# The first eight pairs of tiles take the eight experts' weights where they were prepared in SBUF; the stores to DRAM stand behind

## Chip, cores and metric

One core of one Trainium2 chip. The metric is the device time of one execution in microseconds (us).

## What is computed

A convolution over 7 positions whose weights differ by token and head, and then, on its result, a layer of experts:

```python
w = softmax(weight_gen, axis=-1)                     # 8 x 3584 x 8 heads x 7
out[b, s, h] = sum_k w[b, s, h, k] * x_pad[b, s + k, h]
x = out.reshape(28672, 192)
active = x @ w_skip > 0
e = argmax(x[active] @ w_gate)                       # one of 8 experts
gate = softmax(x[active] @ w_gate)[e]
out[active] = x + gate * (relu(x @ w1[e]) @ w2[e])   # 192 -> 1024 -> 192
```

All is float32 at the kernel's borders. The experts' part runs in float16, each operand split into a high and a low half.

## The kernel before

The 28672 tokens are 16 chunks of 1792; a chunk is four steps. The main loop (`while n["V"] < NCHUNK ...`) takes some 70 steps, and in each it walks a string of tokens, `SEQ[k % 4]`, each of which issues a piece of work if its conditions hold. No scheduler reorders anything: each engine gets its instructions in the order in which the tokens issue them, and waits in that order.

- `a b` (`band`, L323, VectorE) build banded weights; `C G` (`conv`, L342, TensorE) convolve, in two halves; `c e` (`conv_out`, L349, ScalarE) copy the result from PSUM; `K` (`back`, L358, L361) transposes it and forms gate sums, in three PSUM tiles of a pool of three; `O` (`back_out`, L372, L374, ScalarE) copies these out. `O` stands first in a step and takes the `K` of the step before; between the two stands one `F`.
- `L l H R r W V` compute each token's expert and its place (`logits_out` is L389, `rank` L431) and `place` (to L470) writes the rows' addresses; `pop` in `F` then issues 16 scatters of the chunk to the experts' buckets in DRAM (`send`, L483, GpSimd). They wait for TensorE's progress (`scatter`).
- `P` (`prepare`) drives `prep_expert`: for each of 8 experts load two raw halves (L198), take the maximum on ScalarE (L207, whose throw-away output goes into the expert's own weight slot `wo`), reduce it across partitions on TensorE (L213, L219) and VectorE (L215 to L229), write float16 halves into `wo` (L235 to L243), and store them to `wsp` in DRAM by six transfers (L246 to L249). The third block of 1024 columns is moved between partitions by these stores.
- `M` (`assign_one`) picks for the next pair of tiles (256 rows) the prepared expert with most rows waiting; `PAIRS_AFTER` limits the pairs by the chunks that are scattered. `D` (`ahead`, `fetch`) reads the numbers back on SyncE, loads the rows (`xg`, L619) behind the chunk's scatters, and loads the expert's weights from `wsp` into a slot (`wst`, four of them, L631, three transfers).
- `F` (`advance`) runs the pair's layer in eight parts: `prep_rows` (L641 to L664) scales and transposes the rows, `up` (L676, four groups of ten matmuls) and `hh`, `hl` (L680, L686), `down` (L696, four groups of twelve), `finish` (L702) and scatters of the result (L707). A pair that is next starts LEAD = 5 ticks (one per `F`) after its fetch; an assignment is fetched BEHIND = 2 ticks after it was made. When none is ready the stream drains and starts again.

There are 57 pairs: 48 in the loop, 9 dealt at its end. Behind the loop a tail runs the pairs that are left. The slots, PSUM and DRAM tiles carry their dependencies automatically; a load from `wsp` at a register's address counts as touching all of it, so stores and loads of `wsp` wait for each other.

Of the kernel before, what the change touches and what calls it, by code (L numbers as in the profile page):

```python
# [20 lines left out]
P = 128  # L21
# [35 lines left out]
]  # L57
EARLY, EVERY = 5, 2
# [4 lines left out]
LEAD = 5  # L63
BEHIND = 2
# [11 lines left out]
def conv_moe_kernel(ctx, tc, x, wg, w_skip, w_gate, w, out):  # L76
# [34 lines left out]
    wsp = dram.tile([E, P, WC], F16, name="wsp")  # L111
# [30 lines left out]
    nc.vector.tensor_tensor(pick, pick, iof[:, 0:E].unsqueeze(1).to_broadcast([1, E, E]), op=ALU.add)  # L142
    ecap_i = cst.tile([P, E], I32, name="ecap_i")
# [31 lines left out]

    dummy = cst.tile([P, RW], F32, name="dummy")
# [11 lines left out]
    nc.vector.tensor_copy(heads[:, 0, :], iof[:, 0:E])  # L188
# [5 lines left out]
    nc.vector.memset(most[:, E:E + 1], E * TT * float(P) - 0.5)  # L194

# [5 lines left out]
    def prep_expert(e, raws):  # L201
# [18 lines left out]
        yield  # L220
        mv = st.tile([P, 2], F32, tag="wmv", name="wmv")
# [10 lines left out]
        bh, bl = wo[:, 2 * FF:5 * FF // 2], wo[:, 5 * FF // 2:3 * FF]  # L232
# [11 lines left out]
        yield  # L244
        for i in range(2):
            nc.sync.dma_start(wsp[e, 0:64, 2 * FF + i * FF // 2:2 * FF + (i + 1) * FF // 2], bh[64 * i:64 * (i + 1), :])  # L246
            nc.sync.dma_start(wsp[e, 64:P, 2 * FF + i * FF // 2:2 * FF + (i + 1) * FF // 2], bl[64 * i:64 * (i + 1), :])
        nc.sync.dma_start(wsp[e, :, 0:2 * FF], wo[:, 0:2 * FF])
        nc.sync.dma_start(wsp[e, :, 3 * FF:], wo[:, 3 * FF:])  # L249

    prepared, open_, prepares = [0], [0], [0]

    def prep_all():
        raws = [load_part(0, 0), load_part(0, 1)]
        yield
        for e in range(E):
            after = [load_part(e + 1, i) for i in range(2)] if e + 1 < E else []
            yield from prep_expert(e, raws)
            raws = after
            prepared[0] += 1  # L260
            yield
# [256 lines left out]
    def assign(T, F, final):  # L518
# [43 lines left out]
        nc.vector.tensor_scalar(so[:, :, 0], ef, float(E - 1), None, op0=ALU.min)  # L562
# [7 lines left out]
        todo.extend((so, i, T, None) for i in range(F))  # L570
        told.extend([tick[0] + BEHIND] * F)

    def assign_one(T):

        n = prepared[0]
# [4 lines left out]
        nc.vector.scalar_tensor_tensor(t[:, 0:E], t[:, 0:E], float(E), pick[:, n, :] if n < E else iof[:, 0:E],  # L580
# [19 lines left out]
        todo.append((so, 0, T, counted[0]))  # L600
        told.append(tick[0] + BEHIND)

# [8 lines left out]
    def fetch(so, i, T, upto):  # L611

        NT = P * T
        er = nc.values_load(so[0:1, i, 0:1], engines=[ET.SP], min_val=0, max_val=E - 1,
# [119 lines left out]
    def pairs():  # L734

        while True:
# [4 lines left out]
            if ready[0][3] + LEAD > tick[0] and not auto[0]:  # L741
                return
# [3 lines left out]
    def flow():  # L746
# [25 lines left out]
        while cur:  # L772
            py = ps_y.tile([P, 2, 256], F32, tag="py", name="py")
            new = None
            for f2 in range(NFB // 2):
# [16 lines left out]
                if new and f2 == 1:  # L792
                    next(new[1])
# [215 lines left out]
```

## Time and profile before

| | |
|---|---|
| three runs | 964.08, 965.21, 965.73 us; median 965.21 |
| profiled execution | 956.43 us, of which the span is 954.5 |
| mean granted clock of TensorE | 0.927 of 2.4 GHz |
| TensorE busy | 814.2 us (85%) |
| VectorE, ScalarE, GpSimd busy | 659.5 (69%), 474.3 (50%), 403.9 us (42%) |

The page and the timeline come from the profiled execution, which is 8.8 us shorter than the median of the runs. A busy share is a mean over stretches with different limits: TensorE is busy far less in the first third than after it.

### The profile page before, as it was taken

What the parts mean: (1) busy time and instruction counts of PE and PEld (TensorE: products, weight loads), DVE (VectorE), ACT (ScalarE), POOL (GpSimd) and SP (SyncE); (2) the same over time, 40 slices, a digit from 0 to 9 for tenths busy, and PEclk for the clock granted to TensorE, in tenths of its full rate; (3) what the DMA queues carried; (4) which work ended last, traced back from release to release, by engine and by line L of the source; (5) the groups of instructions that cost most, each with busy time, mean ns of one, the idle gap of its engine ahead of it and who ended that gap; (6) DMA issues with size and microseconds to landing.
All of it is one profiled execution on the core that took longest, in us unless ns stands there. A gap on an engine that the chain in (4) does not pass through costs nothing. (4 is left out here: it accounts for less than half of the span.)

```text
span 954.5 us, 36775 instructions
## 1 busy us (share of the span) xinstructions
PE 814.2 (85%) x15248; PEld 694.1 (73%) x15248; DVE 659.5 (69%) x1945; ACT 474.3 (50%) x1141; POOL 403.9 (42%) x415
## 2 busy tenths in 40 slices
PE   0567853778799997999899998999999899999997
PEld 0446633567587886888788786887888789899996
DVE  4888974746877785878686876687675566855553
ACT  0456655454555544555445463555555455455552
POOL 1008883243344536354626372545454353712122
PEclk9787775877799997999999999999999999999999
DMA  6588698897687569576868595768576559876540
GB/s 225 179 291 280 223 305 300 303 323 237 193 283 269 187 229 307 169 246 229 261 190 274 174 299 166 245 201 263 189 267 201 164 196 287 272 257 219 194 158 19
DMA packets 99176, 221.33 MB, mean 232 GB/s; under 512 B 16144, under 2 KB 54859, under 8 KB 97216
## 3 DMA queue, kind: packets, MB, share of 16 engines
q1 hardware_dynamic: 81248, 197.22, 62.2%
q0 software_dynamic: 17760, 21.75, 7.2%
q8 instruction: 120, 1.97, 0.8%
q14 instruction: 48, 0.39, 0.1%
HBM read 152.97 MB, written 77.80 MB: 242 GB/s over the span
## 5 line engine op out<-in xcount | busy, mean ns | idle before, releaser
L483 POOL DMA_INDIRECT bucket<-acc,ixi x256 | 279.2, 1091 | 320.9 <-DVE wst L229 68.0
L676 PE MATMUL ph<-xT,wst 128*128 128x256 f16 x2280 | 296.7, 279 | 20.2 <-DVE hl L686 12.8
L676 PEld LDWEIGHTS <-wst 128*128 128x128 f16 x2280 | 219.8, 100 | 59.5 <-issue 22.4
L680 ACT ACTIVATE hh<-ph 128x512 f16<-128x512 f32 x228 | 135.8, 595 | 243.3 <-PE ph L676 239.9
L686 DVE SCALAR_TENSOR_TENSOR hl<-ph,hh 128x512 f16<-128x512 f32 x228 | 155.8, 684 | 144.6 <-ACT hh L680 144.4
L696 PE MATMUL py<-wst,hh 128*128 128x192 f16 x1824 | 247.0, 248 | 0.0
L696 PE MATMUL py<-wst,hl 128*128 128x192 f16 x912 | 225.6, 247 | 2.8 <-issue 1.9
L707 POOL DMA_INDIRECT out_dram<-xg x114 | 117.1, 1027 | 225.5 <-DVE xg L702 171.7
L342 PE MATMUL bt<-bd,xt 64*32 64x56 f32 x8192 | 125.7, 232 | 59.3 <-DVE bd L323 27.9
L696 PEld LDWEIGHTS <-hh 128*128 128x128 f16 x1824 | 164.3, 99 | 15.8 <-issue 9.4
L342 PEld LDWEIGHTS bt<-bd,xt 64*32 64x32 f32 x8192 | 100.9, 113 | 92.2 <-issue 47.3
L323 DVE TENSOR_TENSOR bd<-rot,mask 128x896 f32<-128x896 f32 x128 | 137.0, 1080 | 8.8 <-DMA rot<-img 8.8
L696 PEld LDWEIGHTS <-hl 128*128 128x128 f16 x912 | 89.8, 98 | 3.4 <-issue 2.1
L664 ACT COPY xT<-pt 128x512 f16<-128x512 f16 x114 | 61.4, 590 | 57.2 <-PE pt L663 57.2
L702 DVE SCALAR_TENSOR_TENSOR xg<-py,fc,xg 128x192 f32<-128x192 f32 x114 | 42.2, 411 | 64.7 <-PE py L696 60.6
L349 ACT COPY xs<-bt 128x448 f32<-128x448 f32 x128 | 66.0, 539 | 37.0 <-PE bt L342 36.8
L358 PE MATMUL pa<-ident,xs 128*112 128x128 f32 x512 | 77.8, 298 | 1.6 <-ACT xT L664 1.1
L650 ACT ACTIVATE xs<-xg,rs 128x192 f16<-128x192 f32 x114 | 45.7, 449 | 44.1 <-DVE rs L647 31.0
L358 PEld LDWEIGHTS pa<-ident,xs 128*112 128x112 f32 x512 | 63.1, 147 | 5.1 <-ACT xT L664 2.8
L663 PE MATMUL pt<-ident,xs 128*128 128x128 f16 x456 | 41.7, 226 | 24.0 <-ACT acc L372 13.2
L372 ACT COPY acc<-pa 112x384 f32<-112x384 f32 x128 | 55.0, 481 | 1.6 <-PE pa L358 1.5
L663 PEld LDWEIGHTS <-xs 128*128 128x128 f16 x456 | 30.1, 100 | 31.1 <-DVE xs L656 19.7
(152 smaller groups left out, 734.3 us busy)
## 6 DMA issues: line engine op xcount, KB each, us to landing
wst<-wsp SPq DMA_DIRECT2D x114, 512.0 KB
wst<-wsp SPq DMA_DIRECT2D x57, 520.0 KB
xt<-in_x_dram SPq DMA_DIRECT2D x64, 384.0 KB
out_dram<-acc SPq DMA_DIRECT2D x16, 1358.0 KB
raw<-in_moe_w_dram SPq DMA_DIRECT2D x16, 768.0 KB
xg<-bucket SPq DMA_DIRECT2D x57, 194.0 KB
rot<-img SPq DMA_DIRECT2D x16, 448.0 KB
wt<-in_weight_gen_dram SPq DMA_DIRECT2D x16, 392.0 KB
```

The source lines that it names most:

```text
L323: nc.vector.tensor_tensor(bd.rearrange("p h (m u) -> p h m u", m=K), rot_[c][:, :, i0 * H:(i0 + 2) * H].rearrange("p m h -> p h m").unsque ...
L342: mm = nc.tensor.matmul(bt[a][GP * j:GP * (j + 1), c0:c0 + QH], xt[p0:p1, b0:b0 + GP], bd_[k, i // 2][p0:p1, i % 2 * H + h, :], start=True ...
L349: nc.scalar.copy(xs_[k][:, 2 * a:2 * a + 2, :], bt_[k][a][:, 0:2 * QB * QH].rearrange("p (x c) -> p x c", x=2))
L358: nc.tensor.transpose(pa[j][0:Q, x * P:(x + 1) * P], xs[:, x, j * Q:(j + 1) * Q], ident)
L483: i = nc.gpsimd.indirect_dma_start(out=bviews[t], out_offset=bass.IndirectOffsetOnAxis(ap=rt_[c][:, t:t + 1], axis=0), in_=acc_[c][:, t, : ...
L663: nc.tensor.transpose(pt[:, 2 * i2 + i, :], xs[:, t, i2, i * P:(i + 1) * P], ident16)
L664: nc.scalar.copy(xT[:, :, t * P:(t + 1) * P], pt)
L676: mm = nc.tensor.matmul(ph[:, fi * 2 * P:(fi + 1) * 2 * P], wt[:, a * FF + f0:a * FF + f0 + P], xT[:, cc, :], start=j == 0, stop=j == 4)
L680: nc.scalar.activation(hh, ph, AF.Relu)
L686: nc.vector.scalar_tensor_tensor(hl, ph, 0.0, hh, op0=ALU.max, op1=ALU.subtract)
L696: mm = nc.tensor.matmul(py[:, t, 0:D], l[:, a], w2v[:, f, r, :], start=f == 0 and t == 0 and j == 0, stop=f == NFB - 1 and j == 2, skip_gr ...
L707: i = nc.gpsimd.indirect_dma_start(out=oviews[nsc[0] % 8], out_offset=bass.IndirectOffsetOnAxis(ap=xg[:, t0 + t, D + 1:D + 2].bitcast(I32) ...
```

## The change

- The first eight assignments name experts 0 to 7 in order, whatever waits in the buckets (`only`), and their pairs use the slot in which that expert was prepared (`fresh`): no load. Experts 4 to 7 are prepared only when pair 0 to 3 is done with its slot (`spent`).
- A new token `s`, once a step from step 14 on, stores one prepared expert, by three transfers, to its own view of `wsp`. Later loads name the stores that they wait for. Four small transfers inside SBUF (from a scratch `low`) do the move between partitions.
- The maximum's throw-away output goes to a scratch `spare`; the slot is taken later.
- `O` stands right behind `K`.
- In a pair's second quarter the rows' low half (L653, L656) is issued before `hl` (L686), not behind it.
- The first pair waits longer: BEHIND 4 and LEAD 7 ticks. Preparation may run faster after step 14 (EVERY 3).

```diff
 SEQ = [
-    "O x F C a D F G w P L F l D c b T M P F e 2 P F H P F D P T M K F P",
+    "x F C a D F G w P L F l D c b T M P F e 2 P F H P F D P s T M K O F P",
...
-EARLY, EVERY = 5, 2
+EARLY, EVERY = 5, 3
+SLOTS = 4
+CUTS = ((0, 2 * FF), (2 * FF, 4 * FF), (4 * FF, WC))
-LEAD = 5
-BEHIND = 2
+LEAD, BEHIND = (5, 7), (2, 4)
...
-    wsp = dram.tile([E, P, WC], F16, name="wsp")
+    wsp = dram.tile([E * P, WC], F16, name="wsp")
+    wviews = dram_disjoint_views(wsp[:, :], E)
+    stored = []
...
+    nc.sync.dma_start(wsp[0:1, 6 * FF + 2:WC], zero[0:1, 0:15].bitcast(F16))
...
     def prep_expert(e, raws):
-        wo = sl.tile([P, WC], F16, tag="wst", name="wst", bufs=4)
         for i in range(2):
-            nc.scalar.activation(wo[:, 0:3 * FF // 2], raws[i], AF.Abs, accum_out=m[:, i:i + 1])
+            nc.scalar.activation(spare, raws[i], AF.Abs, accum_out=m[:, i:i + 1])
             yield
         yield
-        yield
+        if e < SLOTS - 1:
+            yield
...
         nc.tensor.matmul(pm[:, 2 * P:2 * P + 2], ones2, dg, start=True, stop=True)
         yield
+        wo = sl.tile([P, WC], F16, tag="wst", name="wst", bufs=SLOTS)
...
-        bh, bl = wo[:, 2 * FF:5 * FF // 2], wo[:, 5 * FF // 2:3 * FF]
+        low = sl.tile([P, FF], F16, tag="low", name="low", bufs=1)
+        bh, bl = low[:, 0:FF // 2], low[:, FF // 2:]
...
         for i in range(2):
-            nc.sync.dma_start(wsp[e, 0:64, ...], bh[64 * i:64 * (i + 1), :])
-            nc.sync.dma_start(wsp[e, 64:P, ...], bl[64 * i:64 * (i + 1), :])
-        nc.sync.dma_start(wsp[e, :, 0:2 * FF], wo[:, 0:2 * FF])
-        nc.sync.dma_start(wsp[e, :, 3 * FF:], wo[:, 3 * FF:])
+            half = slice(2 * FF + i * FF // 2, 2 * FF + (i + 1) * FF // 2)
+            nc.sync.dma_start(wo[0:64, half], bh[64 * i:64 * (i + 1), :])
+            nc.sync.dma_start(wo[64:P, half], bl[64 * i:64 * (i + 1), :])
+        fresh[e] = wo
+        unkept.append((e, wo))
+
+    def keep():
+        e, wo = unkept.pop(0)
+        to = wviews[e][e * P:(e + 1) * P, :]
+        stored.append([nc.sync.dma_start(to[:, c0:c1], wo[:, c0:c1]).ins for c0, c1 in CUTS])
...
         for e in range(E):
+            while e >= SLOTS and spent[0] <= e - SLOTS:
+                yield
...
-    def assign_one(T):
-        n = prepared[0]
+    def assign_one(T, own):
+        n = len(stored)
+        which = only[:, own, :] if own is not None else pick[:, n, :] if n < E else iof[:, 0:E]
...
-        told.append(tick[0] + BEHIND)
+        told.append(tick[0] + BEHIND[given[0] == 1])
...
+        if own is not None:
+            return T, fresh.pop(own), xg
-        wt = sl.tile([P, WC], F16, tag="wst", name="wst", bufs=4)
-        for c0, c1 in ((0, 2 * FF), (2 * FF, 4 * FF), (4 * FF, WC)):
-            nc.sync.dma_start(wt[:, c0:c1], wsp[ds(er, 1), :, c0:c1].rearrange("a p c -> p (a c)"))
+        wt = sl.tile([P, WC], F16, tag="wst", name="wst", bufs=SLOTS)
+        for c0, c1 in CUTS:
+            i = nc.sync.dma_start(wt[:, c0:c1], wsp[ds(er, P), c0:c1])
+            if paced[0]:
+                for j in chain(*stored[:most_e]):
+                    after(i, j, "the weights of an expert")
...
     def ahead(n):
-        while ... and fetched[0] - before[1] < 4 - (prepared[0] < E):
+        while ... and (todo[0][5] < prepared[0] if todo[0][5] is not None else prepared[0] == E and fetched[0] - before[1] < SLOTS):
...
+                if new and f2 == 1:
+                    next(new[1])
                 late.append((cur, py, f2, up_low(*h)))
...
-                if new and f2 == 1:
-                    next(new[1])
...
-        if ffn[0] is None and ready and ready[0][3] + LEAD <= tick[0] and START <= step[0]:
+        if ffn[0] is None and ready and ready[0][3] + LEAD[spent[0] == 0] <= tick[0] and START <= step[0]:
...
-                chores.append(assigned())
+                chores.append(assigned(given[0] - 1 if given[0] <= E else None))
+        elif t == "s":
+            if unkept and k >= FIRST:
+                keep()
```

How the order moves, in three places. First SyncE around the first pair's fetch (`xg<-bucket`); `wsp<-wst` is a store of weights, `wst<-wsp` a load, `xt` an input of the convolution, `rot` its weights. Before:

```order
L276 DMA xt_131<-in_x_dram 128x768
L316 DMA rot<-img_78 128x7x128
L614 TENSOR_LOAD bs
L616 TENSOR_LOAD bs
L619 ISA
L619 DMA xg<-bucket 128x2x194
L631 ISA
L631 DMA wst<-wsp 128x2048
L631 ISA
L631 DMA wst<-wsp 128x2048
L631 ISA
L631 DMA wst<-wsp 128x2080
```

Now:

```order
L267 DMA wsp<-wst 128x2048 x2
L267 DMA wsp<-wst 128x2080
L297 DMA xt_135<-in_x_dram 128x768
L337 DMA rot<-img_78 128x7x128
L639 TENSOR_LOAD bs
L642 ISA
L642 DMA xg<-bucket 128x2x194
L267 DMA wsp<-wst 128x2048 x2
L267 DMA wsp<-wst 128x2080
L297 DMA xt_136<-in_x_dram 128x768
```

The three loads behind the fetch are gone, and stores of experts 0 and 1 stand on its two sides. Further on the four transfers `wst<-low` of experts 4 to 7 each stand behind a pair's fetch.

ScalarE around the first pair, whose first instruction is the one that reads `xg`. Before:

```order
L372 COPY acc<-pa 112x2x192 x2
L374 COPY ls<-pl 128x224
L240 ACTIVATE wst<-raw,wsc 128x8x192
L641 ACTIVATE xs,S_2525<-xg 128x192 x2
L389 COPY L<-lt 112x4x2x9 x2
L349 COPY xs_2536<-bt 128x448
L650 ACTIVATE xs<-xg,rs 128x192 x2
L349 COPY xs_2536<-bt 128x448
L207 ACTIVATE wst,wm<-raw 128x1536 x2
L372 COPY acc<-pa 112x2x192 x2
```

Now:

```order
L410 COPY L<-lt 112x4x2x9 x2
L370 COPY xs_2494<-bt 128x448 x2
L393 COPY acc<-pa 112x2x192 x2
L395 COPY ls<-pl 128x224
L669 ACTIVATE xs,S_2559<-xg 128x192 x2
L448 ACTIVATE dl<-dl 112x128
L678 ACTIVATE xs<-xg,rs 128x192 x2
L463 COPY qf<-rk 128x136
L370 COPY xs_2668<-bt 128x448 x2
L692 COPY xT<-pt 128x4x128 x2
```

The copies of the logits, of the convolution and of the next `back` now stand ahead of the pair's first instruction, not behind it, and no preparation of an expert stands between.

VectorE in the second quarter of a pair (`xs<-xs` ends the rows' low half, `bd` is a band of the convolution). Before, and then now:

```order
L702 SCALAR_TENSOR_TENSOR xg<-py,fc,xg 128x192 x2
L686 SCALAR_TENSOR_TENSOR hl<-ph,hh 128x512
L653 SCALAR_TENSOR_TENSOR xs<-xg,rs,xs 128x192 x2
L656 COPY xs<-xs 128x2x64 x2
L323 TENSOR_TENSOR bd<-rot,mask 128x896
L686 SCALAR_TENSOR_TENSOR hl<-ph,hh 128x512
```

```order
L730 SCALAR_TENSOR_TENSOR xg<-py,fc,xg 128x192 x2
L681 SCALAR_TENSOR_TENSOR xs<-xg,rs,xs 128x192 x2
L684 COPY xs<-xs 128x2x64 x2
L714 SCALAR_TENSOR_TENSOR hl<-ph,hh 128x512
L344 TENSOR_TENSOR bd<-rot,mask 128x896
L714 SCALAR_TENSOR_TENSOR hl<-ph,hh 128x512
```

The first `hl` has moved behind the rows' low half.

On TensorE the groups of up and down matmuls stand in these steps (a step is counted from one `back` to the next); nine transposes of pairs and two groups of logits lie in steps 16 to 26 in both:

| step | 16 | 17 | 18 | 19 | 20 | 21 | 22 | 23 | 24 | 25 | 26 | sum | 30 | 31 |
|---|---|---|---|---|---|---|---|---|---|---|---|---|---|---|
| up, before | 3 | 3 | 3 | 3 | 0 | 4 | 3 | 4 | 3 | 3 | 4 | 33 | 1 | 2 |
| up, now | 1 | 3 | 4 | 3 | 4 | 1 | 2 | 3 | 4 | 3 | 4 | 32 | 2 | 1 |
| down, before | 0 | 3 | 4 | 5 | 0 | 1 | 4 | 3 | 3 | 4 | 3 | 30 | 3 | 0 |
| down, now | 0 | 2 | 3 | 4 | 3 | 4 | 0 | 3 | 3 | 4 | 3 | 29 | 4 | 0 |

From step 40 on the two orders are never more than a group or two apart.

## Rows read from the trace of the kernel before

**Rows 1.** The page: its first line.
```profile
span 954.5 us, 36775 instructions
```
**Rows 2.** Stretch, us, then busy PE, PEld, DVE, ACT, POOL (xcount); PEclk, DMA share, GB/s.
```profile
148.35:320.50 172.15, 132.69 (x2444) 108.53 (x2444) 116.90 (x336) 85.32 (x196) 61.68 (x67) 0.84 0.81 270
234.30:259.60 25.30, 17.87 (x379) 13.51 (x378) 21.66 (x71) 14.36 (x34) 9.76 (x11) 0.80 0.60 187
357.50:382.10 24.60, 19.15 (x381) 15.41 (x379) 12.77 (x38) 10.08 (x29) 14.51 (x14) 0.79 0.90 306
```
**Rows 3.** Timeline of TensorE, undisturbed work: start, us, line, [idle before <-releaser].
```profile
102.19 1.09 PE L358 MATMUL pa<-ident,xs 128*112 128x128 f32 x8
...
104.67 1.90 PE L342 MATMUL bt<-bd,xt 64*32 64x56 f32 x126 [0.66 <-ACT xs L349]
106.50 1.08 PE L358 MATMUL pa<-ident,xs 128*112 128x128 f32 x8
...
843.39 0.22 PE L663 MATMUL pt<-ident,xs 128*128 128x128 f16 x1
...
844.19 1.25 PE L676 MATMUL ph<-xT,wst 128*128 128x256 f16 x10
845.29 0.33 PE L696 MATMUL py<-wst,hh 128*128 128x192 f16 x2
...
846.28 1.25 PE L676 MATMUL ph<-xT,wst 128*128 128x256 f16 x10
```
**Rows 4.** Timeline of TensorE around the first pairs and after the dry spell.
```profile
129.39 2.10 PE L342 MATMUL bt<-bd,xt 64*32 64x56 f32 x128 [4.54 <-DMA xt<-in_x_dram]
...
145.35 3.19 PE L381 MATMUL lt<-four,ls 128*112 128x32 f32 x16 [0.48 <-ACT acc L372]
...
158.13 0.97 PE L361 MATMUL pl<-xs,gt 128*32 128x224 f32 x8 [7.84 <-ACT L L389]
163.27 0.27 PE L663 MATMUL pt<-ident,xs 128*128 128x128 f16 x1 [4.17 <-ACT acc L372]
...
198.22 2.29 PE L676 MATMUL ph<-xT,wst 128*128 128x256 f16 x10 [2.57 <-ACT xs L349]
...
371.45 0.97 PE L663 MATMUL pt<-ident,xs 128*128 128x128 f16 x8 [3.59 <-ACT acc L372]
```
**Rows 5.** Timeline of SyncE around the first fetch.
```profile
144.32 0.63 SPq L316 DMA_DIRECT2D rot<-img  x1
154.45 0.41 SPq L619 DMA_DIRECT2D xg<-bucket  x1
```
**Rows 6.** Timeline of GpSimd: chunk 2's last scatter.
```profile
151.30 0.94 POOL L483 DMA_INDIRECT bucket<-acc,ixi  x1 [0.30 <-issue]
```
**Rows 7.** Timeline of ScalarE around the first pairs.
```profile
157.05 0.36 ACT L641 ACTIVATE xs<-xg 128x192 f16<-128x192 f32 x1 [9.65 <-DMA xg<-bucket]
...
195.69 1.48 ACT L207 ACTIVATE wst<-raw 128x1536 f16<-128x1536 f32 x1 [6.26 <-PE py L696]
```
**Rows 8.** Waits of TensorE, 120 to 270 us: total us, times, longest.
```profile
PE ph L676 <- DVE hl L686: 4.6, 3, 2.7
...
PE pl L361 <- DVE wmv L222: 4.2, 3, 2.1
...
PE pm L219 <- DVE wd L217: 2.2, 3, 0.9
```
**Rows 9.** Sum of the five stretches of 139.6 to 252.2 at 1.2 GHz.
```profile
sum 64.90, PE 43.59 PEld 32.80 DVE 40.80 ACT 29.81 POOL 17.30; mean PE 8.72 PEld 6.56 DVE 8.16 ACT 5.96 POOL 3.46
```
**Rows 10.** Waits of TensorE in the tail, 775 to 950 us.
```profile
PE pt L663 <- DVE xs L656: 3.3, 17, 0.3
```
**Rows 11.** Timeline of VectorE in a step of the steady loop.
```profile
501.39 0.74 DVE L653 SCALAR_TENSOR_TENSOR xs<-xg,rs,xs 128x192 f16<-128x192 f32 x2
502.16 0.29 DVE L656 COPY xs<-xs 128x128 f16<-128x128 f16 x2
```
**Rows 12.** Timeline of TensorE in the same step.
```profile
501.53 1.26 PE L676 MATMUL ph<-xT,wst 128*128 128x256 f16 x10 [0.62 <-DVE hl L686]
```

More of the change, by code (lines that the diff above doesn't have):

```diff
@@ L142, in conv_moe_kernel @@
     nc.vector.tensor_tensor(pick, pick, iof[:, 0:E].unsqueeze(1).to_broadcast([1, E, E]), op=ALU.add)
+    only = cst.tile([1, E, E], F32, name="only")
+    nc.gpsimd.memset(only, -BIG)
+    nc.gpsimd.affine_select(out=only, in_=only, compare_op=ALU.not_equal, fill=0.0, base=0,
+                            pattern=[[1, E], [-1, E]], channel_multiplier=0)
+    nc.vector.tensor_tensor(only, only, iof[:, 0:E].unsqueeze(1).to_broadcast([1, E, E]), op=ALU.add)
     ecap_i = cst.tile([P, E], I32, name="ecap_i")
@@ L194, in conv_moe_kernel @@
     nc.vector.memset(most[:, E:E + 1], E * TT * float(P) - 0.5)
+    spare = cst.tile([P, 3 * FF // 2], F16, name="spare")
     def load_part(e, i):
@@ L561, in assign @@
         yield
-        nc.vector.tensor_scalar(so[:, :, 0], ef, float(E - 1), None, op0=ALU.min)
+        nc.vector.tensor_scalar(so[:, :, 0], ef, float(E - 1), float(P), op0=ALU.min, op1=ALU.mult)
         yield
@@ L569, in assign @@
         yield
-        todo.extend((so, i, T, None) for i in range(F))
-        told.extend([tick[0] + BEHIND] * F)
-    def assign_one(T):
-        n = prepared[0]
+        todo.extend((so, i, T, None, E, None) for i in range(F))
+        told.extend([tick[0] + BEHIND[0]] * F)
+    def assign_one(T, own):
+        n = len(stored)
+        which = only[:, own, :] if own is not None else pick[:, n, :] if n < E else iof[:, 0:E]
         w = float(P * T)
@@ L579, in assign_one @@
         yield
-        nc.vector.scalar_tensor_tensor(t[:, 0:E], t[:, 0:E], float(E), pick[:, n, :] if n < E else iof[:, 0:E],
+        nc.vector.scalar_tensor_tensor(t[:, 0:E], t[:, 0:E], float(E), which,
                                        op0=ALU.mult, op1=ALU.add)
@@ L599, in assign_one @@
         yield
-        todo.append((so, 0, T, counted[0]))
-        told.append(tick[0] + BEHIND)
+        todo.append((so, 0, T, counted[0], n, own))
+        told.append(tick[0] + BEHIND[given[0] == 1])
     def together(*gs):
@@ L609, in together, with fetch @@
                     gs.remove(g)
-    def fetch(so, i, T, upto):
+    def fetch(so, i, T, upto, most_e, own):
         NT = P * T
-        er = nc.values_load(so[0:1, i, 0:1], engines=[ET.SP], min_val=0, max_val=E - 1,
+        if own is None:
+            er = nc.values_load(so[0:1, i, 0:1], engines=[ET.SP], min_val=0, max_val=(E - 1) * P,
                             skip_runtime_bounds_check_because="clamped to the experts on the chip")
@@ L725, in ahead @@
     def ahead(n):
-        while len(ready) < n and todo and (told[0] <= tick[0] or auto[0]) and (todo[0][3] is not None or not unsent) and fetched[0] - before[0] < XG and fetched[0] - before[1] < 4 - (prepared[0] < E):
+        while len(ready) < n and todo and (told[0] <= tick[0] or auto[0]) and (todo[0][3] is not None or not unsent) and fetched[0] - before[0] < XG and (todo[0][5] < prepared[0] if todo[0][5] is not None else prepared[0] == E and fetched[0] - before[1] < SLOTS):
             fetched[0] += 1
@@ L740, in pairs @@
                 return
-            if ready[0][3] + LEAD > tick[0] and not auto[0]:
+            if ready[0][3] + LEAD[0] > tick[0] and not auto[0]:
                 return
@@ L837, in chosen, with assigned @@
         n["h"] += 1
-    def assigned():
-        yield from assign_one(TT)
+    def assigned(own):
+        yield from assign_one(TT, own)
         asked[0] -= 1
```

6 lines of the change are left out of this document (2 added, 4 removed), and 6 rows, old and new, of the table SEQ.

## The prediction, made before the changed kernel ran

> **What bounds the kernel now.** I read the page first, then TensorE's busy time by stretches, then its timeline where stretches are thin, then the rows of whoever it waited for. All sums are against the profiled execution: 956.4 us, of which the span is 954.5 [rows 1]; the median of the runs shown is 965.2, 8.8 above it, and I add 8.8 at the end.
>
> A step of the main loop is, on TensorE, the stretch from one `back` (L358) to the next. Undisturbed work has fixed prices [rows 3]: a step with no pair in it takes 106.50 − 102.19, less 0.66 idle, 3.65 us; one group of ten up matmuls 845.29 − 844.19 = 1.10; one group of twelve down matmuls 846.28 − 845.29 = 0.99; a pair's transposes 844.19 − 843.39 = 0.80; the logits 3.19 at 1.2 GHz [rows 4], so 1.6 at 2.4.
>
> The stretch 148.35 to 320.50 (steps 16 to 26) is where the pairs begin and the experts 4 to 7 are prepared between them. It lasts 172.15 us at a granted clock of 0.84 [rows 2]. By the table of groups its work is 11 × 3.65 + 33 × 1.10 + 30 × 0.99 + 9 × 0.80 + 2 × 1.6 = 40.2 + 36.3 + 29.7 + 7.2 + 3.2 = 116.6 us. So **55.5 us are lost there**. The reader is to see four kinds of loss in the rows:
> - The entrance. SyncE issued its last transfer at 144.32 and stood until 154.45 before the first pair's rows [rows 5], because that fetch waits for the scatters of chunk 2, and GpSimd's last one began at 151.30 [rows 6]. ScalarE stood 9.65 us at L641 for those rows [rows 7], and behind it stood the copies that TensorE needed: 7.84 us idle before L361, then 4.17 before the pair's transposes for a copy of L372 [rows 4].
> - ScalarE stood 6.26 us at L207 for a pair's down matmuls [rows 7]: the throw-away output of the maximum goes into a weight slot, which that pair still held. TensorE then lost 2.57 to L349, queued behind it [rows 4].
> - A drain between pairs: 25.30 us in steps 20 and 21 [rows 2].
> - The clock: 64.9 us of 139.6 to 252.2 went at 1.2 GHz, with TensorE busy for 43.59 of them [rows 9].
>
> **The change, part by part.** *Loads and stores.* Eight fetches of weights (3 transfers each) go; the eight stores become 3 transfers instead of 6, behind the pairs, and four small copies inside SBUF take the place of those of the third block. I cost the traffic itself at nothing on the path, because no row of TensorE names a weight load; the work that hides it is the stream of up and down matmuls. What it can free is the one wait of a convolution for `xt`, 4.54 us [rows 4], when loads, stores and scatters overlapped. Bounds 0 and 4.5; I take **3**, nearer to the row, since three experts' stores now stay away until step 14.
>
> *Steps 16 to 26.* By the table the change issues 32 up and 29 down groups here, 114.5 us of work by the same prices; the 2.1 us less come later and cancel. What stays lost:
> - Entrance: the scatters are neither moved nor fewer, so the rows cannot be there before about 157 [rows 5, 6, 7]. Behind them stand a few small steps, between 2 us and the 6.2 from 157.05 to 163.27 [rows 4, 7]; I take 3, since the order now puts the copies of L389 and L349 ahead of the wait. From 148.35 to 160.2 is 11.9, with 3.65 of work: 8 lost, and 6 more for the half clock that follows. **14.**
> - The drain, now between pairs 3 and 4 (steps 21 and 22, while expert 4 is prepared in the slot that pair 0 leaves). I price it by the one before: 25.3 less its work, 2 × 3.65 + 4 × 1.10 + 0.99 + 2 × 0.80 = 14.3. **11.**
> - The preparation on TensorE's path: 4.2 and 2.2 us for three experts [rows 8], 2.1 each, four experts. **8.5.**
> - Waits for `hl`: 4.6 [rows 8], as they are. **4.6.**
>
> Together 38 of 55.5, so the gain is **17**. From below it is 0 (each wait finds a successor); from above 38 (all but the drain and a bare entrance of 6 go).
>
> A rule to weigh here: in the rows, 43.59 us of busy time at 1.2 GHz would be 21.8 at 2.4, so the clock alone can give back at most 21.8 [rows 9], part of which is in my 17. The Trainium skill's "TensorE: Matmul & The Clock Gate" (HAM oscillation — how this bites in real kernels) counts the penalty as the whole throttled time × (1 − 1.2/2.4). By it an estimate for the 64.9 us is 32.5, and with that in place of the 17 the sum would end 15 us lower; the trace speaks against the full figure, since TensorE was idle for a third of that time.
>
> *Copies right behind transposes.* `back_out` follows `back` at once. Beside the 4.17 above, the transposes after the dry spell at 357.5 waited 3.59 for such a copy [rows 4]. Those two steps took 24.60 [rows 2] for 2 × 3.65 + 3 × 1.10 + 3 × 0.99 + 0.80 + 1.6 = 16.0 of work. The order keeps the dry spell (3 up and 4 down groups), so I take **4**, the wait and little of the clock; bounds 0 and 8.6.
>
> *The low half ahead of `hl`.* In the second quarter of a pair VectorE now runs L653 and L656 before L686. In the tail this ends the wait of the transposes for `xs`: 3.3 us in 17 waits [rows 10]; **3**, bounds 0 and 3.3. In the main loop it is a cost. Where the third up group stands between the halves of a convolution it waits for that very `hl` (0.62 at 501.53 [rows 12]), which now ends 502.16 + 0.29 − 501.39 = 1.06 later [rows 11]. In the order of the change five such groups follow after step 23: **−5**; bounds 0 and −9, if other pairs join.
>
> *The rest.* One more constant, a few set-up instructions and one tiny store at the start: **−0.5**, bounds 0 and −1. Views, scratch and the address in rows instead of experts are free; pairs 0 to 7 even save one register load each.
>
> Sum: 3 + 17 + 4 + 3 − 5 − 0.5 = 21.5. 956.4 − 21.5 = 934.9; with 8.8, **944**.
>
> **The rivals.**
> - *Only the named waits go* (the scratch's 2.57, part of 4.17; 5 of my 17, and nothing at the dry spell). VectorE, busy 116.90 of 172.15 us [rows 2], carries the same preparation later and takes over. Sum 3 + 5 + 3 − 5 − 0.5 = 5.5: **960**. For it: the entrance is set by scatters. Against it: ScalarE's two stalls, 9.65 and 6.26, leave work queued that nothing else held. Chance 0.18.
> - *The clock stays up* from the first pair on: with 38 in the stretch and 8.6 at the dry spell the sum is 47, so **918**. For it: the clock was 1.2 GHz just where the waits stood. Against it: the drain and the entrance remain. Chance 0.06. It is the case nearest to what that rule of the Trainium skill (same page and section) would give.
> - *Slower: SyncE holds back the copies of the third block.* In the order, each expert's four copies stand behind a pair's fetch. If a fetch waits for scatters as the first one did (144.95 to 154.45, 9.5 us [rows 5]), expert and pair are late by that, for four experts 38 us: 21.5 − 38 = −16.5, so **982**. It decides once more than two of the four fetches stand that long, 2.3 × 9.5 being the gain. Against it: later pairs are told only after the chunk's last scatter was issued. Chance 0.10.
> - *No effect* (the loss stays 55 us, the steps merely change places): 965. Chance 0.04.
>
> **How the numbers follow.** The forecast has 0.62. The range of 924 to 963 takes in its own bounds where most of them lie (20 us to either side) and the first rival; it leaves out the clock's rival, the slower one and no effect, 0.20. Two parts in a thousand, about 2 us, are what a measurement can tell from no change. Faster: 0.62 × 0.97 + 0.18 × 0.9 + 0.06 = 0.82. Slower: 0.10 and a little of the forecast's worst end, 0.12. Within: 0.06.
>
> **What would show it.** In the changed profile: ScalarE's maximum (before L207) waits for no down matmul; no wait of transposes for L372's copies; steps 16 to 26 take about 155 us; one drain between pairs 3 and 4, with 1.2 GHz; in the tail no wait of the transposes for `xs`. I am wrong if the first pair's rows arrive well before 155 us, if the clock stays at 2.4 GHz from the first pair on, or if SyncE's copies of the third block stand behind a fetch.

## The result, and the profile after

The changed kernel took **948.73 us** (median of six runs, 946.41 to 960.81), beside 960.88 for the kernel before: a ratio of 0.988 [0.984, 0.992]. Ratios compare fast runs alone, and the run of 960.81 was a slow one. Measured again, with the profile that is read below, it was 953.75 beside 962.93: 0.990 [0.986, 0.993]. So it is faster, by 9 to 12 us where the sum had 21. The experiments ran on three chips. On that of the first four (this second measurement among them) the kernel before took 962.93 us, on that of the next four 962.16, so times of these eight are set side by side. On the third chip, where the last four ran, it took 1120.23 us, some 16% more; times of that chip are compared among themselves only, and with the others by their ratios to before.

The profiled execution of the change took 955.03 us, 1.3 above its median. That of before (956.43) lay 6.5 *below* the 962.93 of its runs beside the second measurement, so the two traces differ by less than the kernels do. I therefore read them by stretches. "Step k" is the stretch from one `back` on TensorE (now L379) to the next, counted from 0. The version "without own slots" is an experiment below; its profiled execution (966.08) is near its own median, and so is that of the best version (942.54), which is an experiment too.

| TensorE, us | before | change | change without own slots | best version |
|---|---|---|---|---|
| to step 16 | 148.4 | 144.5 | 153.9 | 146.9 |
| steps 16 to 26 | 172.1 | 164.7 | 166.3 | 158.6 |
| steps 27 to 47 | 266.0 | 272.5 | 272.0 | 262.0 |
| steps 48 to 62 | 182.6 | 193.3 | 193.8 | 192.6 |
| from step 63 to the span's end | 185.4 | 178.1 | 178.4 | 180.5 |
| span | 954.5 | 953.1 | 964.4 | 940.6 |

The change is 11.3 us ahead at the end of step 26 (309.2 against 320.5), loses that and more from there to step 62, and wins 7.3 in the tail. Of the 11.3, 2.1 is work that comes later (32 up and 29 down groups are issued by then, 33 and 30 in before; 30 and 27 in the best version, whose 158.6 is to be read so). First the page of the change, then its stretches, with the same columns as [rows 2], which the first and the last of them answer:

```profile
span 953.1 us, 36734 instructions
```
```profile
144.50:309.20 164.70, 128.51 (x2426) 105.18 (x2426) 114.36 (x329) 91.62 (x202) 69.51 (x73) 0.85 0.73 242
213.40:247.90 34.50, 26.33 (x602) 21.35 (x600) 26.48 (x78) 19.78 (x40) 7.39 (x8) 0.95 0.70 245
309.20:581.70 272.50, 249.76 (x4874) 212.96 (x4873) 198.09 (x596) 135.05 (x341) 129.55 (x126) 0.96 0.70 226
337.60:367.60 30.00, 25.17 (x576) 21.45 (x574) 18.35 (x54) 10.59 (x24) 19.05 (x18) 0.93 1.00 343
581.70:775.00 193.30, 176.96 (x3408) 151.72 (x3407) 129.21 (x409) 96.17 (x248) 87.65 (x89) 0.98 0.64 209
```

The stretches of before that are not in [rows 2]:

```profile
320.50:586.50 266.00, 247.72 (x4852) 210.43 (x4851) 194.97 (x589) 131.66 (x340) 128.60 (x126) 0.96 0.70 229
586.50:769.10 182.60, 172.31 (x3387) 147.97 (x3386) 127.42 (x407) 93.01 (x243) 85.81 (x87) 1.00 0.66 219
```

In steps 16 to 26 TensorE's idle time (stretch less busy) went from 39.5 to 36.2 us, and the granted clock from 0.84 to 0.85: nearly nothing of either. In 48 to 62 the change has 6.0 us more idle time and a clock of 0.98 where before had 1.00.

Now the entrance of the change, on GpSimd, SyncE, ScalarE and TensorE, which answers [rows 4 to 7]:

```profile
154.79 0.94 POOL L504 DMA_INDIRECT bucket<-acc,ixi  x1 [0.30 <-issue]
```
```profile
141.08 0.92 SPq L337 DMA_DIRECT2D rot<-img  x1
157.16 0.42 SPq L642 DMA_DIRECT2D xg<-bucket  x1
```
```profile
159.88 0.36 ACT L669 ACTIVATE xs<-xg 128x192 f16<-128x192 f32 x1 [12.05 <-DMA xg<-bucket]
```
```profile
141.62 3.09 PE L402 MATMUL lt<-four,ls 128*112 128x32 f32 x16 [1.49 <-ACT acc L393]
...
149.32 1.02 PE L363 MATMUL bt<-bd,xt 64*32 64x56 f32 x64
161.88 0.29 PE L691 MATMUL pt<-ident,xs 128*128 128x128 f16 x1 [11.54 <-ACT xs L678]
```

The form of the wait is new, its length is not: where before stood 7.84 and 4.17 us for copies that were queued behind the rows, the transposes now stand 11.54 us for the rows themselves. The fetch (157.16) still follows the last scatter (154.79) at once, and that scatter begins 3.5 us later than in before, though step 16 begins 3.9 earlier. So the first transposes come at 161.88 where they came at 163.27. Then the waits of TensorE from 120 to 270 us [rows 8], and in the tail [rows 10]:

```profile
PE pt L691 <- ACT xs L678: 14.0, 2, 11.5
PE pm L230 <- DVE wd L228: 6.9, 3, 4.3
...
PE bt L363 <- DVE hl L714: 2.5, 1, 2.5
...
PE ph L704 <- DVE hl L714: 1.8, 1, 1.8
...
PE pl L382 <- DVE wmv L234: 1.2, 1, 1.2
```
```profile
PE pt L691 <- DVE xs L684: 0.7, 1, 0.7
```

### The profile page after: what moved, and what is told of

Its sections match the earlier page's. It is cut to its first block, busy times and chain, and to the rows that moved or that the text cites. A ratio compares the mean times of both kernels' runs of the same rounds, so it can differ in the third digit from the quotient of the medians.

```text
span 958.9 us, 36734 instructions
## 1 busy us (share of the span) xinstructions
PE 819.6 (85%) x15248; PEld 701.5 (73%) x15248; DVE 660.9 (69%) x1946; ACT 479.5 (50%) x1141; POOL 409.6 (43%) x417
## 5 line engine op out<-in xcount | busy, mean ns | idle before, releaser
L504 POOL DMA_INDIRECT bucket<-acc,ixi x256 | 283.7, 1108 | 283.6 <-PE bt L363 71.6
L704 PE MATMUL ph<-xT,wst 128*128 128x256 f16 x2280 | 297.6, 279 | 23.5 <-DVE hl L714 13.6
L704 PEld LDWEIGHTS <-wst 128*128 128x128 f16 x2280 | 220.1, 100 | 63.6 <-issue 23.8
L724 PE MATMUL py<-wst,hh 128*128 128x192 f16 x1824 | 251.5, 251 | 0.0
L724 PE MATMUL py<-wst,hl 128*128 128x192 f16 x912 | 227.9, 250 | 0.2 <-DVE hl L714 0.2
L363 PE MATMUL bt<-bd,xt 64*32 64x56 f32 x8192 | 128.6, 234 | 67.8 <-DVE bd L344 28.0
L724 PEld LDWEIGHTS <-hh 128*128 128x128 f16 x1824 | 166.3, 100 | 16.1 <-issue 7.7
L379 PE MATMUL pa<-ident,xs 128*112 128x128 f32 x512 | 79.1, 302 | 6.4 <-issue 5.1
L379 PEld LDWEIGHTS pa<-ident,xs 128*112 128x112 f32 x512 | 64.3, 149 | 10.0 <-issue 5.6
L691 PE MATMUL pt<-ident,xs 128*128 128x128 f16 x456 | 37.1, 225 | 14.8 <-ACT xs L678 11.5
L669 ACT ACTIVATE xs<-xg 128x192 f16<-128x192 f32 x114 | 40.2, 360 | 11.4 <-DMA xg<-bucket 11.3
```

The source lines that it names most:

```text
L363: mm = nc.tensor.matmul(bt[a][GP * j:GP * (j + 1), c0:c0 + QH], xt[p0:p1, b0:b0 + GP], bd_[k, i // 2][p0:p1, i % 2 * H + h, :], start=True ...
L379: nc.tensor.transpose(pa[j][0:Q, x * P:(x + 1) * P], xs[:, x, j * Q:(j + 1) * Q], ident)
L504: i = nc.gpsimd.indirect_dma_start(out=bviews[t], out_offset=bass.IndirectOffsetOnAxis(ap=rt_[c][:, t:t + 1], axis=0), in_=acc_[c][:, t, : ...
L704: mm = nc.tensor.matmul(ph[:, fi * 2 * P:(fi + 1) * 2 * P], wt[:, a * FF + f0:a * FF + f0 + P], xT[:, cc, :], start=j == 0, stop=j == 4)
L724: mm = nc.tensor.matmul(py[:, t, 0:D], l[:, a], w2v[:, f, r, :], start=f == 0 and t == 0 and j == 0, stop=f == NFB - 1 and j == 2, skip_gr ...
```

## Experiments

My theory after the first reading: own slots bring the gain at the first pairs, and the other edits move the places where the order leaves TensorE without a pair. The rival: each edit acts by the waits that it removes. What the order gives can be counted before any run. Groups of ten up matmuls in each of steps 16 to 37:

```
before             3 3 3 3 0 4 3 4 3 3 4 3 4 3 1 2 4 3 4 3 4 3
change             1 3 4 3 4 1 2 3 4 3 4 3 4 3 2 1 4 3 4 3 4 3
without own slots  1 3 4 3 1 2 4 3 4 3 4 3 4 3 2 1 4 3 4 3 4 3
before, O moved    3 4 3 2 1 4 3 4 3 4 3 4 3 3 0 4 3 4 3 4 3 4
change, O back     0 4 3 4 3 2 0 4 3 4 3 3 4 3 4 3 4 3 3 4 3 4
O back, prep early 0 4 3 4 3 3 3 0 4 3 4 3 3 4 3 4 3 4 3 3 4 3
O back, LEAD 5     3 3 3 4 3 0 3 3 3 4 3 4 3 4 1 2 3 4 3 4 3 4
```

A dry spell is a step or two in which the order has few groups or none. Each row has one in steps 19 to 23. All but two rows have a second one in steps 30 and 31. The best version below has the row of `O` back.

**The change again** (no edit).

> The changed kernel once more, beside the others, for a second profile. Theory (the gain arises in steps 16 to 26, is given back in part in the main loop by waits for hl, and comes again in the tail): ratio to before about 0.988, steps 16 to 26 some 8 us shorter than before, a pair of the tail 8.77 us instead of 9.13, and in 385 to 775 us some 16 us of TensorE's waits for hl where before had 9. Rival (what was lost after step 24 in the first profile was chance stalls with no releaser, the issue waits): the waits for hl fall back to 9 us and the main loop takes no longer than before.

Measured: 953.75 (ten runs), 0.990 [0.986, 0.993]. The theory held: steps 16 to 26 are 7.4 us shorter than before, a pair of the tail takes 8.77 us instead of 9.13, and TensorE's waits for `hl` between 385 and 770 us are 16.5 us where before had 9.0.

**`hl` first everywhere.** The low half of the rows goes back behind `hl`, in the loop and in the tail:

```diff
-                if new and f2 == 1:
-                    next(new[1])
...
+                if new and f2 == 1:
+                    next(new[1])
```

> The change without its low half ahead of hl: hl first again, in the loop and in the tail. Theory: the order costs about 10 us in the main loop (waits for hl 16.5 against 9.0 us) and gives 0.36 us for each of 17 pairs of the tail, 6 us; without it the time is about 4 us below the change, 944 to 946 where the change has 948.7. Rival (the order costs nothing in the loop): 6 us above the change.

Measured: 953.13, 0.992 [0.987, 0.996]: neither 4 us below the change nor 6 above it, but the same. The trace shows both effects, and they cancel. Its steps 48 to 62 and its tail, where the change has 193.3 and 178.1 us:

```profile
578.40:766.60 188.20, 177.74 (x3410) 152.09 (x3408) 128.28 (x408) 96.36 (x248) 86.60 (x89) 0.98 0.65 214
766.60:951.20 184.60, 172.29 (x1859) 159.16 (x1856) 105.39 (x350) 89.49 (x222) 60.20 (x64) 0.99 0.59 196
```

**Low half first in the tail alone:**

```diff
-                if new and f2 == 1:
+                if new and f2 == 1 and auto[0]:
...
+                if new and f2 == 1 and not auto[0]:
+                    next(new[1])
```

> The low half ahead of hl in the tail alone, hl first in the main loop. Theory: both gains, some 10 us below the change, 938 to 941. Rival (no cost in the loop): the same time as the change within 2 us.

Measured: 952.53, 0.988 [0.984, 0.992]. The change's waits of TensorE between 385 and 770 us, then this version's:

```profile
PE ph L704 <- DVE hl L714: 10.5, 9, 1.9
PE bt L363 <- issue: 8.9, 4, 3.1
PE bt L363 <- DVE hl L714: 6.0, 6, 1.2
```
```profile
PE bt L363 <- issue: 11.5, 4, 3.8
PE ph L704 <- DVE hl L714: 4.2, 8, 0.9
PE bt L363 <- DVE hl L714: 2.9, 6, 0.8
```

The waits for `hl` fall from 16.5 to 7.1 us, as the order says, and of the 10 us that I expected nothing is seen beyond the interval; 2.6 us come back as waits without a releaser. In steps 48 to 62 this version is 3.2 us shorter than the change (190.1), in steps 27 to 47 it is 2.1 longer (274.6). Neither of the two versions differs from the change beyond its interval.

**`O` back.** The copies stand at the start of the next step again, in all four rows of `SEQ`; all else as changed:

```diff
-    "x F C a D F G w P L F l D c b T M P F e 2 P F H P F D P s T M K O F P",
+    "O x F C a D F G w P L F l D c b T M P F e 2 P F H P F D P s T M K F P",
```

> The change with the copies of back_out at the start of the next step again, as before. Theory (they removed 4.2 + 3.6 us of waits of transposes and free PSUM earlier): 4 to 8 us above the change. Rival (right behind the transposes ScalarE itself stands for TensorE, 10.4 us of idle time before L393 in the first profile against 1.5 before, and holds back what is behind): the same as the change or up to 5 us below it.

Measured: **945.98**, 0.984 [0.981, 0.988]; 7.8 us below the change on the same chip, where even the rival had at most 5. Between the transposes of pairs 10 and 11 now lie 13.0 us, where the change has 30.0. Steps 27 to 47, in which that spell lay, took 266.3 us instead of 272.5, with three more up groups in them.

**`O` moved, alone.** The kernel before, with `O` behind `K`; the diff is the one above read backwards.

> The kernel before with one edit: the copies of the convolution's transposed rows (O) stand right behind the transposes (K), where the change puts them, and not at the start of the next step. Taken back in the changed kernel, this edit gained 7 us (946 against 953). Theory: it is a loss wherever it stands, since it moves the point in the step at which the order opens the next pair by a third of a step, so that the spell without a pair at steps 31 and 32 becomes a whole step; the time is 2 to 8 us above before's, ratio 1.002 to 1.008. Rival: alone it frees the transposes of their wait for the accumulator copies (3.6 us at 371 and 4.2 us at 163) and costs nothing else: ratio 0.995 to 0.998; the loss in the changed kernel was then the meeting with the own slots.

Measured: 973.57, **1.011 [1.007, 1.015]**: slower than before by 10 to 11 us, more than the theory had. So this edit is a loss on either kernel. The reason that the theory gives is not borne out. In the order the edit does empty a whole step (step 30: no group) where before had two thin ones, but between the transposes of pairs 10 and 11 lie 23.8 us here and 28.1 in before. Nor did the edit, alone, end the waits at which it was aimed. The transposes' waits from 120 to 270 us, before and here:

```profile
PE pt L663 <- ACT acc L372: 7.2, 2, 4.2
```
```profile
PE pt L663 <- ACT acc L372: 6.2, 2, 4.2
```

What costs the 10 us stays open.

**All but the own slots.** Pairs 0 to 7 fetch their experts again, stores at the preparation, and an expert's preparation no longer waits for a pair to be done with its slot. The maximum's scratch `spare`, `O`, low half, LEAD and BEHIND are as changed; the scratch `low` for the third block goes, though the expectation says that it stays. Of the diff, what matters:

```diff
-        if own is not None:
-            return T, fresh.pop(own), xg
...
-        bh, bl = low[:, 0:FF // 2], low[:, FF // 2:]
+        bh, bl = wo[:, 2 * FF:5 * FF // 2], wo[:, 5 * FF // 2:3 * FF]
...
+        nc.sync.dma_start(wsp[e, :, 0:2 * FF], wo[:, 0:2 * FF])
+        nc.sync.dma_start(wsp[e, :, 3 * FF:], wo[:, 3 * FF:])
```

> The change without its main part: the first eight pairs fetch their expert from DRAM again as in the kernel before (three slots while experts are prepared, stores in the step of the preparation, one view of the store); scratch of its own for the halves of the third block, copies right behind the transposes, the low half ahead of hl, LEAD and BEHIND stay as changed. Theory: the own slots and late stores carry the gain, which sits in steps 16 to 26; without them these steps take about 172 us again as before (164.7 changed), pair 3 begins near 240 us (213 changed), and the time lies between the kernel before and 4 us above it, a ratio of 0.999 to 1.005 (the tail's gain of 6 us against some 10 us that the low half ahead of hl and the moved copies cost the loop). Rival: the smaller edits (scratch, copies, low half, LEAD) carry the gain; then the ratio is 0.990, as the change's, and pair 3 begins before 220 us.

Measured: 967.40, **1.005 [1.002, 1.008]**. As the theory had it, the rest without own slots makes the kernel slower, by half a per cent. Pair 3 begins at 245.0 (213.4 in the change). What I had wrong is where it shows: steps 16 to 26 take 166.3, not 172, but step 16 begins 9.4 us later than in the change. At the end of step 26 the two stand at 320.2 and 309.2, with the same number of groups behind them and all eight experts prepared, and from there on they run alike:

```profile
320.20:592.20 272.00, 250.35 (x4873) 213.56 (x4872) 198.26 (x597) 134.91 (x341) 129.00 (x126) 0.96 0.70 227
592.20:786.00 193.80, 177.33 (x3410) 152.10 (x3408) 129.21 (x409) 96.17 (x248) 87.94 (x89) 0.98 0.64 208
786.00:964.00 178.00, 169.32 (x1859) 159.52 (x1856) 105.37 (x350) 89.63 (x222) 60.49 (x64) 0.99 0.61 203
```

**So own slots, with the late stores and the later preparation that go with them, are worth 11 us beside the other edits, all of it before step 27** (13.6 us by the medians, on two chips; 0.9896 / 1.0052 = 0.984 by the ratios). Which of these parts carries it is not separated. Of the 11 us, 9.4 lie ahead of step 16, before any pair has run: by then five experts are prepared here, as in before, and four in the change, and a convolution waits 5.78 us for `xt` (4.54 in before, none in the change). And in steps 16 to 26 stands a stall that neither before nor the change has: by the profile ScalarE stood 16.07 us for a store of weights to land before it wrote into a slot, and TensorE 17.90 us for the copy that was queued behind it.

```profile
131.21 2.25 PE L343 MATMUL bt<-bd,xt 64*32 64x56 f32 x128 [5.78 <-DMA xt<-in_x_dram]
...
182.38 1.15 ACT L236 ACTIVATE wst<-raw,wsc 128x1024 f16<-128x1024 f32 x1 [16.07 <-DMA wsp<-wst]
...
185.58 2.29 PE L677 MATMUL ph<-xT,wst 128*128 128x256 f16 x10 [17.90 <-ACT xT L665]
```

**`O` back and low half first in the tail alone** (the two diffs together).

> The changed kernel with two of its edits taken back: the copies O stand at the start of the next step as before, and the low half of the activations stands ahead of hl in the tail alone, not in the loop of convolution steps. Theory: the waits of up matmuls for hl between 385 and 770 us fall from 17 us to 7, and part of this reaches the end, as the spell without a pair between pairs 10 and 11 is gone: 940 to 943 us, 3 to 6 below the version with O taken back alone (946). Rival: TensorE's waits on hl there are only the form that a limit elsewhere takes, as it was in the two kernels with hl first, where waits without a releaser took their place: 945 to 947.

Measured: **942.36**, 0.980 [0.975, 0.984], the best of all. Its waits for `hl` between 385 and 770 us are 9.1. Against `O` back alone, measured on the other chip, it is 3.6 us, within the intervals, so that part is not shown. Steps 27 to 47 hold 72 up groups here and 69 in the change, and still take 10.5 us less:

```profile
305.50:567.50 262.00, 249.02 (x4935) 213.17 (x4933) 201.03 (x605) 135.47 (x349) 124.35 (x126) 0.99 0.73 236
```

Idle time is 13.0 us against 22.7 and the granted clock 0.99 against 0.96. The clock goes with the second dry spell in every trace but those of the third chip (in these steps 0.95 to 0.97 with it, 0.98 and 0.99 without). The idle time does not (18.1 us with `O` back alone, 21.1 in the next experiment), so that the spell cost it is not shown.

**The same, with the fifth expert's loads and maximum not waiting for its slot.** The wait now stands ahead of the reduction across partitions, shortly before the slot is taken:

```diff
+        while e >= SLOTS and spent[0] <= e - SLOTS:
+            yield
         open_[0] = 1
         pm = ps_s.tile([P, 512], F32, tag="s", name="pm")
...
-            while e >= SLOTS and spent[0] <= e - SLOTS:
-                yield
```

> As the version with O and the loop's order of the low half taken back, with one edit more: the preparation of an expert waits for a free slot only where it takes the slot, so that the fifth expert's loading and its maximum run while the fourth pair still computes. Theory: the spell between pairs 3 and 4 (34 us from transposes to transposes, 17 would be a pair's pace) waits for that preparation, and shortens by 8 to 12 us: 933 to 938 us in all, at least 5 below the version without this edit. Rival: the spell hangs on the order (the next pair's rows are opened only at a fixed place of the next step) or on the assignment behind the pair, and moves by a step without getting shorter: within 3 us of the version without it.

Measured: 946.13, 0.983 [0.979, 0.987], no better than without the edit. The rival was right that the spell moves and does not get shorter: 35.3 us between pairs 3 and 4 become 19.1, and 20.9 between pairs 4 and 5 become 29.6. Pair 6 begins at 280.4, where it began at 279.9.

**Stores at the preparation,** own slots kept:

```diff
-        unkept.append((e, wo))
+        unkept.append((e, wo)); keep()
```

> The changed kernel with the stores of each expert taken back to the place where it is prepared (right behind the copies of its third block), instead of a step each from the first pair on; the own slots stay, and TensorE's order is the same. Theory: what gains is that a first pair does not fetch what lies in a slot, not that the stores come late: the stores stand in the setup's steps, where SyncE waits some 2 us per expert for the copies of the third block, and the first transposes (161.9 us) come 0 to 3 us later; the time is within 4 us of the change's 953.8, ratio 0.988 to 0.994. Rival: the late stores carry several us, since SyncE and the DMA engines are needed for the image at that time: 958 to 962, ratio 0.995 to 1.0.

Measured, on the third chip: 0.985 [0.980, 0.991]; the change, on another chip, had 0.990. That the stores come late is worth nothing that shows here. For the other chips this does not settle it: on the third no convolution waits for `xt` up to step 16 in the kernel before either, where TensorE has other waits (last section), so what late stores could free there is not on TensorE's path.

**LEAD and BEHIND of the first pair taken back,** on the best version:

```diff
-LEAD, BEHIND = (5, 7), (2, 4)
+LEAD, BEHIND = (5, 5), (2, 2)
```

> The version with O and the loop's order of the low half taken back (942 us), with the longer waits ahead of the first pair taken back too: LEAD 5 and BEHIND 2 ticks for all pairs. Theory: the order then opens the first pair a step earlier than its rows can be there (they hang on the scatters of the third chunk, which end at 156 us), so TensorE stands at the first pair's transposes, which begin no earlier than 160 us: nothing gained, 942 to 948. Rival: the entrance hangs on these ticks, the first transposes come at 150 to 156 us and the time falls by 4 to 8 us, to 934 to 938.

Measured, on the third chip: 1.001 [0.997, 1.005], where the best version had 0.977. Both theories fail. The first transposes do come earlier, at 187.3 us against 193.5, and nothing of it reaches the end. The second dry spell is back in the order. These are the stretches between the transposes of pairs 10 and 11, of this version and of the best one:

```profile
391.40:433.00 41.60, 30.69 (x593) 24.04 (x591) 25.55 (x79) 11.50 (x27) 20.04 (x21) 0.91 0.83 288
```
```profile
397.00:415.40 18.40, 16.27 (x242) 12.95 (x241) 7.52 (x24) 7.41 (x19) 7.86 (x9) 0.81 0.50 168
```

This spell does not make the whole 2.4%. The version with stores at the preparation, on the same chip, has it too (33.7 us between the same transposes) and came to 0.985. Here pair 11 begins 17.6 us later than in the best version, pair 38 7.2 and pair 47 14.0. Where the rest goes is open. But the edit counts: with own slots and late stores in place, the kernel without the first pair's longer wait is no faster than before.

**The best version again.**

> The version with O and the loop's order of the low half taken back, again, beside the kernel before with five more rounds: ratio 0.976 to 0.984 if the first measurement (0.9797) was right; a rival is that it was a lucky set of runs: 0.985 to 0.99, no better than the change itself.

Measured, on the third chip: 0.977 [0.971, 0.982], as in the first measurement.

**The kernel before against itself.**

> The kernel before against itself, with a profile of its own: what the measurement calls no change, and a second trace of before, as the first trace's execution (956.4) lies 5 to 6 us under the median of all its runs (961 to 963). Theory: the ratio is 1.000 within 0.004, and the new execution, if it lies near 962, has its additional time in the loop of convolution steps (385 to 770 us), where waits without a releaser and granted clock differ between executions, not in steps 16 to 26, which take 172 us again within 2. Rival: the additional time lies in steps 16 to 26 (over 175 us); then the gain there was more than the two first traces show.

Measured: 1.001 [0.997, 1.005], no change. The trace came from the third chip, so it can't tell what set the first trace of before apart from the median. That stays open. A hint is in the table: steps 48 to 62 took 182.6 us in that trace and 188.2 to 195.0 in the nine others that are not from the third chip. A part of that is no chance. Before has a group less of each kind there than the change (2.1 us), and the low half shows: the five kernels with `hl` first in the loop took 188.2 to 192.6 us, the four traces with the low half first 193.3 to 195.0.

## Why the prediction was right, and where its sum was not

The direction was right, and the time lay within the range, 4.7 us above the forecast. That it came so near is in part luck: the sum started from 965.2 us, and the kernel before measured 960.9 over all six runs. Against the runs of before beside it, the gain was 12.2 and 9.2 us, not 21.5. By the prediction's own steps:

- **Loads, stores and set-up (+3, −0.5).** No convolution waits for `xt` at the place of the 4.54 us any more, and step 16 begins 3.9 us earlier. The number is right, but one expert's preparation has moved behind step 16 too, which the term did not count. And what it won ended at the first pair's rows, which were read 2.8 us later than in before (159.88 for 157.05).
- **Steps 16 to 26 (+17): this is the term that was mis-sized.** The stretch took 164.7 us, 7.4 less than before, and 2.1 of that is work that comes later. So the loss fell by 5.3, from 55.5 to 50.2 us (164.7 less 114.5 of work), where I had 38. The step that failed is "together 38 of 55.5", in two places. The entrance: the rows hang on the last scatter, and from the start of step 16 to the first transposes TensorE was idle 11.8 of 17.4 us, where I had 8 lost; in before it was 12.0. The half clock: busy time exceeds the work by 128.5 − 114.5 = 14.0, of which I had charged 6, at the entrance alone; before it was 132.7 − 116.6 = 16.1. The two make 11.8 of the 12.2 us that were missing.
- The other three items came out near: 6.9 us for the preparation (8.5; the 1.2 at L382 lies ahead of step 16), 1.8 + 2.5 = 4.3 for `hl` (4.6, which counted the up matmuls alone), and for the drain between pairs 3 and 4, 34.5 less 24.2 of work (three steps, five up and seven down groups, one pair's transposes) = 10.3 (11). There is luck in it. The drain holds 2.5 of the waits for `hl` and 2.0 of those for the preparation, so they are counted twice. The price of a preparation was misread: the window of [rows 8] begins at 120 us and takes in five experts, and in before's steps 16 to 26, which hold three, these waits are 3.0 us. And the drain's granted clock was 0.95, not the 1.2 GHz that was to show it.
- **Copies right behind transposes (+4): the sign was wrong.** In the change the waits of the transposes for the copies did go (none is left from 120 to 270 us). But taking the edit back gained 7.8 us, and alone it costs 10. I priced the wait and not what the order does with a shifted `F`: I read that it "keeps the dry spell", which it does (30.0 us between pairs 10 and 11 for 28.1), and did not ask whether the old place of `O` would have lost it (13.0).
- **Low half ahead of `hl` (tail +3, loop −5).** In the tail the wait is gone but for 0.7 us of 3.3, and pairs follow each other in 8.77 us instead of 9.13, which over 17 pairs is 6 us, twice the term; the wait of the transposes was not all that the edit ended. In the loop the waits for `hl` between 385 and 770 us are 16.5 against 9.0, 7.5 more. In steps 48 to 62 the low half first took 193.3 and 195.0 us where `hl` first took 188.2 or 190.1, and 192.6: 2 to 5 us, near the term. The two effects cancel.
- **The rivals.** *Only the named waits go* (5.5 us) was nearer than the forecast in the size of the gain and in its terms: 5 for steps 16 to 26, where 5.3 was won, and nothing at the dry spell. Its mechanism, VectorE taking over, is not shown: TensorE's waits for its `wd` in these steps rose from 0.9 to 6.9 us, but with four preparations for three. *The clock stays up*: no, 0.85 for 0.84. The rule of the Trainium skill beside it ("TensorE: Matmul & The Clock Gate", HAM oscillation — how this bites in real kernels) would price the slow clock by its time alone; the row that bears on it is the excess of busy time over work, 16.1 us before, less than even the 21.8 that the row allowed. *SyncE holds back the copies*: no. Only the first fetch stood long, and the copies of the third block waited for their own preparation, as SyncE's waits from 120 to 270 us show:

```profile
SPq L259 <- ACT low L250: 35.4, 4, 13.9
SPq L642 <- DMA bucket<-acc,ixi: 13.7, 3, 11.4
```

- **The base.** I added 8.8 us for the distance of the profiled execution from its median. As a distance of totals that was fair (6.5 in the second measurement), but a sum of terms against one fortunate execution hides that the change was compared, stage by stage, with steps 48 to 62 as no other trace shows them.

## What to carry to other kernels

Where the program fixes the order, count the work in each step of the order before pricing a wait: in the changed kernel an edit had removed every wait at which it was aimed, and taking it back still gained 7.8 us, with an order that has no second dry spell. The count is a start and not the whole: the same edit alone cost 10 us with a shorter spell. When a stretch is priced by a list of its losses, compare the list with the whole loss, idle and slow clock apart; what is not on the list does not go away. And a change of many parts is worth taking apart, each part out of the whole: without own slots and what goes with them nothing was gained (1.005), on the best version nothing without the first pair's longer wait (1.001 for 0.977), and one part, `O`, was a loss; taken back, with the low half in the tail alone, it left a gain nearly twice as large.

## What the runs showed of the hardware

The third chip took 16% longer for the same program (spans 1115.3 and 954.5 us), and not on all engines: `hh` on ScalarE took 596 ns a piece (595 before), `hl` on VectorE 684 (684), and in the tail the transposes of the 51st and of the 57th pair, six pairs apart, lay 54.8 us apart on both. What differed were TensorE's short convolution matmuls, L342, which waited without a releaser, and whose busy time grew from 125.7 to 182.9 us. With the waits below that is 134.6 of the 160.8 us. The kernel before in its first trace and on the third chip, matmuls and then weight loads:

```profile
PE bt L342 <- issue: 18.6, 13, 4.0
...
PEld bt L342 <- issue: 47.3, 93, 6.3
```
```profile
PE bt L342 <- issue: 96.0, 209, 2.7
...
PEld bt L342 <- issue: 161.9, 296, 6.8
```

On the timeline the matmuls come in threes and fours, some 0.7 us apart, and then 59 of them in 1.07 us:

```profile
87.24 0.32 PE L342 MATMUL bt<-bd,xt 64*32 64x56 f32 x4 [0.34 <-issue]
87.98 0.27 PE L342 MATMUL bt<-bd,xt 64*32 64x56 f32 x3 [0.43 <-issue]
88.73 0.31 PE L342 MATMUL bt<-bd,xt 64*32 64x56 f32 x4 [0.48 <-issue]
...
97.45 1.07 PE L342 MATMUL bt<-bd,xt 64*32 64x56 f32 x59 [0.41 <-issue]
```

That looks like instructions arriving slowly. The Trainium skill ("Runtime: NRT & Kernel Launch", Instruction fetch mechanics) says that each engine's sequencer fetches its instructions by DMA ahead of need and that this is mostly hidden. No run here shows whether that fetch was what stood. The packets of the profile's instruction queues were as many (120 and 48) and took no larger share of the span (0.8% in the first trace, 0.7% on the third chip), so no slower transfer shows there. The cause is open.
